# Setup copies and the written-out opening order of a fused forgetting-attention and GELU kernel

## Chip, cores and metric

The kernel runs on one core of one Trainium2 chip. The metric is the device time of one execution in microseconds (us), as the median over several executions; the span of a profiled execution goes from its first to its last instruction.

## What is computed

Attention with a forget gate for 8 batches, 8 heads, 576 positions and 64 columns a head, and then a two-layer network with a tanh-GELU on the 4608 x 512 result:

```python
scores = scale * q @ k.T                       # per head, 576 x 576
cum    = cumsum(log(clip(f, 1e-4, 1)))         # along the sequence
scores = where(j > i, -1e9, scores + cum[i] - cum[j])
attn   = softmax(scores)                       # along j
x      = (attn @ v) as 4608 x 512
out    = gelu_tanh(x @ w_in) @ w_out           # 512 -> 2048 -> 512
```

The decay of a row cancels in the softmax. So the kernel needs only a weight exp(-cum[j] - 64) for each key: it multiplies the rows of v by it, and the denominators are products with the column of weights.

## The kernel before

**Tiling.** Four heads make a quad, and there are 16 of them, two for each batch. For a quad, `scores` (L197) multiplies K and Q on TensorE with four 32-row groups side by side into PSUM (tile `ps_s`, pool of two buffers, shared with the first layer's `ps_h`). ScalarE takes the exponential into `pt` (L223). The diagonal blocks are then masked: by `mask` (L225) with GpSimd's affine selects, or by `mask_by_product` (L249) with VectorE, which multiplies by the triangles in `causal`. `denominators` (L292) multiplies `pt` by the weights `w_bf`, transposes, takes reciprocals and transposes again. `attn_out` (L310) multiplies `pt` by the weighted values `vw` and writes `xT`, normalised. `make_vw` (L173) makes `vw` from `v_nat` and `wT`, on GpSimd or VectorE. Quads 0 and 1 are cut into two parts of 256 and 320 query positions (`part` 0 and 1), so that the first layer can begin early.

**The network** works in nine chunks of 512 positions. `mlp_in` (L317) makes 256 of 2048 hidden columns of a chunk, and ScalarE applies the GELU. For chunk 0, `mlp_in_half` (L334) makes 512 hidden columns for one part of the positions. `mlp_out` (L352) is a generator: each step is one 128-row block of the hidden dimension into a block of 128 output rows, after the 16th VectorE copies the result out and SyncE stores it.

**Setup** (L374) issues the load of f on SyncE and the first two K and Q loads on GpSimd, makes an identity and an upper triangle `utri_f32` on GpSimd, and takes the logs of f on ScalarE. Five TensorE transposes put them into `ps_lt`, and two copies (L399, L400) into `logfT`. The running sums are matmuls of `logfT` by the triangle and by ones (`make_w`, L421). The second of them takes `before`, sums of whole blocks, which `sums_before` (L414, `SB`) makes on GpSimd. ScalarE's exponential of the sums gives `wT` (L426). `cast_w` (L445) makes the bf16 copy `w_bf`, and `triangles` (L409) the bf16 triangles.

**The order of the opening** is written out by hand in `FRONT` (L73). Each engine takes its instructions in the order in which the words stand, so a word that waits holds up what stands behind it on its engines. The words, with quad i, batch b, chunk c:

- `TK.i`, `TQ.i`: VectorE transposes of K and Q into `kT`, `qT`. `LK.i`, `LQ.i`: their loads, issued by GpSimd. A buffer holds every second quad.
- `LU.t`: the load of tile t (128 positions) of batch 0's v, all heads; `LV.b.half`: five loads for half of the heads of batch b. SyncE issues them. `WI.c`, `WO.c`: quarters of w_in and w_out, issued by GpSimd.
- `S.i.r`: scores of round r, all four heads; `H.i.r.g`: two of the heads. `M` and `m`: the masks on GpSimd and VectorE. `D.i.part`: denominators. `V.i.x.part`: a product with `vw` and the multiply into `xT`.
- `vw.i`, `VW.i`: `make_vw` on VectorE, GpSimd. `CL.i`: a copy inside `vw`. `CW`: `make_w`. `SB`: `sums_before`. `W`: `cast_w`. `TR`: `triangles`. `Z`: zero fills on GpSimd.
- `J.half.g`: `mlp_in_half`. `I.c.pr`: `mlp_in`. `F.c.n` and `f.c.n`: n steps of `mlp_out` of chunk c, in whole matmuls or, for `f`, as four matmuls of 32 rows.
- `B.n.cols`: n matmuls of zeros (`keep_busy`, L191), whose result nothing reads.
- `word@other`: the word's first DMA is issued only after the last DMA of `other` has landed; the issuing engine waits.

After `FRONT`, a loop over chunks 2 to 8 (L525) does the rest: each turn has the first layer of a chunk, the second layer of the one before, and the attention of two further quads. `TileContext` works out the semaphores; within an engine the order is that of the program (`manual_schedule`).

Of the kernel before, what the change touches and what calls it, by code (L numbers as in the profile page):

```python
# [16 lines left out]
def kernel(  # L17
# [10 lines left out]
    nc = tc.nc  # L28

    B, H, S, D = q.shape  # L30
    BH = B * H
    NT = (S + 127) // 128
# [34 lines left out]
    LOW, HIGH = NT, NT - 1  # L67
# [3 lines left out]
    """  # L71

    FRONT = """  # L73
        TK.0 TQ.0 TK.1 B.3.128 LU.4@LK.0 WO.0 SB CW TQ.1 W S.0.0 B.1.128 TR LU.0 B.4.256 M.0.0 B.2.384 S.0.2 B.4.256 H.1.0.1
        H.1.0.0 D.0.0 H.0.1.1 LU.1 vw.0.0 H.1.1.1 B.3.256 Z m.1.0 vw.1.0 H.0.1.0 LU.2@LK.0 WI.1 V.0.1.0 WI.0@LU.0 M.0.1 D.1.0 LU.3@LU.4 H.1.1.0 WI.3
        WI.2 V.0.0.0 LK.2 H.0.3.1 V.1.1.0 H.0.3.0 vw.0.1 m.0.3 V.1.0.0 H.1.3.0 H.1.3.1 D.0.1 H.1.2.0 M.1.1 M.1.3 LQ.2 H.1.2.1 V.0.0.1 V.0.1.1 D.1.1
        J.0.1 VW.1.1 V.1.1.1 WO.1@LU.3 WO.2 WO.3 LK.3 V.1.0.1 LV.1.1@WO.2 TQ.2 J.0.0 J.1.0 J.0.2 TK.2 J.1.2 J.1.1 J.0.3 J.1.3 F.0.6 LQ.3
        LV.1.0@LQ.3 LK.4 S.2.0 F.0.11 S.2.2 TQ.3 F.0.10 S.2.1 m.2.0 TK.3 TK.4 vw.3 F.0.10 LV.2.0 vw.2 M.2.2 CL.3 M.2.1 S.3.0 LQ.4
        CL.2 LQ.5 f.0.7 D.2 S.3.1 f.0.6 V.2.0 TQ.4 LK.5 S.3.2 f.0.7 m.3.0 V.2.1 S.4.1 F.0.5 H.4.2.1 M.3.1 M.3.2 D.3 H.4.0.0
        H.4.0.1 V.3.1 VW.4 v.3.0 LK.6 TQ.5 LV.3.0@LQ.3 f.0.2 LQ.6 H.4.2.0 TK.5 I.1.1 TK.6 LK.8 CL.4 I.1.6 LK.7 I.1.5 I.1.4 I.1.3  # L80
        m.4.0 I.1.2 I.1.0 I.1.7 F.1.8 M.4.1 TQ.6 S.5.0 LV.2.1@LK.7 M.4.2 f.1.7 VW.5 D.4 S.5.1 F.1.6 F.1.7 S.5.2 LV.3.1 LQ.7 m.5.1
        m.5.0 V.4.0 f.1.5 V.4.1 S.6.0 f.1.4 CL.5 vw.6 M.5.2 D.5 f.1.3 LQ.8 S.6.1 V.5.1 f.1.6 m.6.0 V.5.0 m.6.1 S.6.2 m.6.2
        CL.6 F.1.10
    """

    singles = ctx.enter_context(tc.tile_pool(name="singles", bufs=1))
# [6 lines left out]
    def many(n, shape, dtype, name):  # L93
        return [singles.tile(shape, dtype, name=f"{name}{i}") for i in range(n)]

    ident_f32 = singles.tile([BH, BH], FP32, name="ident_f32")
    utri_f32 = singles.tile([128, 128], FP32, name="utri_f32")
# [8 lines left out]
    vw = many(2, [128, NT + 1, 4, D], BF16, "vw")  # L106
# [6 lines left out]
    logfT = singles.tile([128, NT * BH], FP32, name="logfT")  # L113
    before = singles.tile([128, (NT - 1) * BH], FP32, name="before")
    wT = singles.tile([128, NQ, NT, 4], FP32, name="wT")
    w_bf = singles.tile([128, NQ, NT + 1, 4], BF16, name="w_bf")
    shift = singles.tile([128, 1], FP32, name="shift")
    idle = singles.tile([128, 512], BF16, name="idle")
    causal = many(2, [128, 128], BF16, "causal")


    def after(ins, other):

        tc.add_manual_dep(ins.ins, other.ins.name, mybir.DependencyInfo(
            mybir.DependencyClass.Sync, mybir.DependencyReason.DATA), reason="order of loads")

    def load_v(b, h0=0, nh=H, ts=range(NT)):
        ins = []
        for t in ts:
            n = min(128, S - 128 * t)  # L130
            ins.append(nc.sync.dma_start(
                out=v_nat[b % 2][:n, t, h0:h0 + nh, :],
                in_=v[b, h0:h0 + nh, 128 * t:128 * t + n, :].rearrange("h p d -> p h d"),
            ))
        return ins
# [16 lines left out]
    def load_one(src, dst, i):  # L152
        b, h0 = i // QPB, 4 * (i % QPB)
        return nc.gpsimd.dma_start(  # L154
            out=dst[i % 2].rearrange("p a d -> p (a d)"),
            in_=src[b, h0:h0 + 4].rearrange("h (p a) d -> (h p) (a d)", p=32))
# [217 lines left out]
    def setup():  # L374
        nc.sync.dma_start(out=f_sb, in_=f.rearrange("b h s -> (b h) s"))
        dmas["LK.0"] = load_one(k, k_c, 0)
        dmas["LQ.0"] = load_one(q, q_c, 0)
        make_identity(nc, ident_f32)
        dmas["LK.1"] = load_one(k, k_c, 1)
        dmas["LQ.1"] = load_one(q, q_c, 1)  # L380
        make_upper_triangular(nc, utri_f32, val=1.0, diag=True)

        nc.vector.memset(idle, 0.0)
        nc.vector.memset(ones_f32, 1.0)
        nc.vector.memset(logfT, 0.0)
        nc.vector.memset(shift, -64.0)
        nc.vector.memset(wT[64:128, :, HIGH, :], 0.0)
        for t_ in kT:
            nc.vector.memset(t_[:, 0:64], 0.0)
            nc.vector.memset(t_[:, 64 + S:], 0.0)  # L390
        nc.vector.tensor_scalar(f_sb, f_sb, 1e-4, 1.0, op0=ALU.max, op1=ALU.min)
        nc.scalar.activation(f_sb, f_sb, AF.Ln)
        idle_ps.append(psO.tile([128, 1024], FP32, name="idle_ps", tag="po"))
        ps_lt = psM.tile([128, NT * BH], FP32, name="ps_lt", tag="m")
        for t in range(NT):
            n = min(128, S - 128 * t)
            nc.tensor.transpose(ps_lt[:n, t * BH:(t + 1) * BH], f_sb[:, 128 * t:128 * t + n], ident_f32)
        run(SETUP)
        nc.vector.tensor_copy(logfT[:, :HIGH * BH], ps_lt[:, :HIGH * BH])  # L399
        nc.vector.tensor_copy(logfT[0:64, HIGH * BH:], ps_lt[0:64, HIGH * BH:])  # L400

    def zeros():
        for t_ in v_nat:
# [2 lines left out]
            nc.gpsimd.memset(t_[0:64, LOW, :, :], 0.0)  # L406
        nc.gpsimd.memset(w_bf[0:64, :, LOW, :], 0.0)

    def triangles():  # L409
        for m in causal:  # L410
            nc.vector.tensor_copy(m, utri_f32)
        nc.vector.tensor_copy(causal[1][64:128, 0:64], utri_f32[0:64, 0:64])

    def sums_before(eng):  # L414
        eng.tensor_copy(before[:, 0:BH], logfT[:, 0:BH])
# [23 lines left out]
    dmas = {}  # L439
# [2 lines left out]
        by_columns[:] = [True] * tiled  # L442
        pull(fills.setdefault(c, mlp_out(c)), n)

    def cast_w():  # L445
        nc.vector.tensor_copy(w_bf[:, :, 0:NT, :], wT)
        nc.vector.tensor_copy(w_bf[64:128, :, LOW, :], wT[0:64, :, 0, :])

    def load_values(b, half):
        return load_v(b, 4 * half, 4)  # L450

    ops = {
        "W": cast_w,
        "CW": make_w,
        "SB": lambda: sums_before(nc.gpsimd),
        "sb": lambda: sums_before(nc.vector),
        "Z": zeros,
        "TR": triangles,
        "S": lambda i, r: scores(i, r),
        "H": lambda i, r, g: scores(i, r, ((2 * g, 2 * g + 1),)),  # L460
        "M": lambda i, r, *keys: mask(i, r, keys),
# [10 lines left out]
        "LQ": lambda i: load_one(q, q_c, i),  # L472
        "LV": load_values,
        "LU": lambda t: load_v(0, ts=(t,)),
        "WI": load_w_in,
        "WO": load_w_out,
        "I": lambda c, pr: mlp_in(c, (pr,)),
# [6 lines left out]
    def run(table):  # L484

        for word in table.split():
            word, _, gate = word.partition("@")
            name, *args = word.split(".")
            did = ops[name](*map(int, args))
            did = did if isinstance(did, list) else [did]  # L490
            if gate:
                after(did[0], dmas[gate])
            dmas[word] = did[-1]

    def step(i, j, c, n):

# [25 lines left out]
    with tc.manual_schedule():  # L522
        setup()
        run(FRONT)
        for c in range(2, NCH):  # L525
            for pr in range(2):
                mlp_in(c, (pr,))
            out_part(c - 1, CH)
            if c + 1 < B:
                prepare(2 * c + 3, 2 * c + 4)  # L530
            if c + 2 < B:
                load_v(c + 2)
            for pr in range(2, NP):
# [37 lines left out]
```

## Time and profile before

| | |
|---|---|
| median of nine runs | 349.76 us (343.11 to 355.57) |
| the nine runs | 343.11, 344.15, 344.72, 344.78, 349.76, 350.85, 352.25, 355.29, 355.57 |
| the profiled execution: its own time, its span | 344.17 us, 342.5 us |
| mean granted TensorE clock of the profiled execution | 0.990 |
| DMA | 33.25 MB in 50999 packets, 38992 of them under 512 B |

The page has one line for the busy time of each engine (PE is TensorE's matmuls, PEld its weight loads, DVE VectorE, ACT ScalarE, POOL GpSimd, SP SyncE) and then the span in 40 slices of 8.6 us; a digit is the busy share in tenths. PEclk is the clock granted to TensorE, in tenths of full speed. A line of waits tells who waited for whom, the total in us, how often, and the longest. A line of the table by stretches has the stretch, its length, the busy time of PE, PEld, DVE, ACT and POOL with the number of instructions, the clock, the busy share of the 16 DMA engines (over 1 where packets overlap) and the GB/s that they moved.

### The profile page before, as it was taken

The page shows a single profiled execution, that of the slowest core. Times are in us where ns is not written, and L with a number is a line of the kernel's source. Part 1 is how long each engine was busy: PE and PEld are TensorE (multiplying, and loading weights), DVE is VectorE, ACT ScalarE, POOL GpSimd, SP SyncE. Part 2 cuts the span into 40 slices and gives each one's busy share as a digit, 9 for nine tenths or more (in the row PEclk, how much of TensorE's full clock was granted, in tenths as well). Part 3 has the DMA queues.
Part 4 walks back from the last instruction along what each step waited for, and adds up shares of the span by engine and source line. Part 5 has one row for each costly group of instructions (what it writes and reads, how often), then busy time and mean ns, then how long its engine had stood idle before and what let it go on. Part 6 is the DMA issues. An engine that isn't in the chain of part 4 may idle for free.

```text
span 342.5 us, 9365 instructions
## 1 busy us (share of the span) xinstructions
PE 331.8 (97%) x4221; PEld 163.0 (48%) x4221; DVE 135.7 (40%) x209; ACT 190.8 (56%) x192; POOL 91.4 (27%) x131
## 2 busy tenths in 40 slices
PE   4999999999999999999999999999999999999995
PEld 2448834544454454444444444444444544444443
DVE  5785139670575235343425243514530450011011
ACT  3874576776665566557574667466745714510500
POOL 6565014442110135321642055106500410000000
PEclk9969999999999999999999999999999999999999
DMA  7999975984532930096007710560100010002012
GB/s 129 212 198 200 208 184 108 202 147 92 129 74 70 215 86 34 33 206 134 34 33 166 142 65 33 110 130 33 65 31 2 33 63 32 0 33 83 9 47 77
DMA packets 50999, 33.25 MB, mean 97 GB/s; under 512 B 38992, under 2 KB 41296, under 8 KB 50960
## 3 DMA queue, kind: packets, MB, share of 16 engines
q0 software_dynamic: 7808, 13.63, 23.0%
q1 hardware_dynamic: 43008, 18.96, 20.9%
q8 instruction: 33, 0.54, 0.6%
q10 hardware_dynamic: 144, 0.07, 0.1%
q14 instruction: 6, 0.05, 0.0%
HBM read 36.85 MB, written 9.44 MB: 135 GB/s over the span
## 4 chain that ended last, share of the span: by engine, by line
PE 83%; POOL 1%; ACT 1%; issue 0%; POOLq 0%; DVE 0%
PE pso L363 35%; PE ps_h L325 32%; PE po L283 8%; PE ps_s L215 7%; POOL vw L177 1%; ACT pt L223 1%; PE ps_o L283 0%; POOL pt L229 0%; POOLq L566 0%; DVE o_st L368 0%; POOLq L229 0%
## 5 line engine op out<-in xcount | busy, mean ns | idle before, releaser
L363 PE MATMUL pso<-w_out_sb,gT 128*32 128x512 bf16 (+2 forms) x1483 | 134.7, 377 | 0.0
L223 ACT ACTIVATE pt<-ps_s 128x1024 bf16<-128x1024 f32 (+2 forms) x100 | 94.0, 991 | 39.4 <-PE ps_s L215 36.9
L325 PE MATMUL ps_h<-xT,w_in_sb 128*128 128x512 bf16 x512 | 112.9, 379 | 0.0
L332 ACT ACTIVATE gT<-ps_h 128x1024 bf16<-128x1024 f32 x64 | 65.5, 1023 | 76.2 <-PE ps_h L325 76.2
L363 PEld LDWEIGHTS <-gT 128*32 128x32 bf16 (+1 forms) x1483 | 56.5, 97 | 56.9 <-issue 2.4
L325 PEld LDWEIGHTS <-w_in_sb 128*128 128x128 bf16 x512 | 49.6, 98 | 61.4 <-issue 2.5
L229 POOL TENSOR_SCALAR_AFFINE_SELECT pt<-pt 128x512 bf16<-128x512 bf16 (+3 forms) x62 | 37.6, 617 | 122.1 <-ACT pt L223 120.8
L368 DVE COPY o_st<-pso 128x512 f32<-128x512 f32 (+2 forms) x37 | 24.9, 674 | 90.2 <-PE pso L363 90.0
L215 PE MATMUL ps_s<-qT,kT 32*128 32x64 bf16 (+5 forms) x896 | 37.7, 268 | 0.9 <-ACT pt L223 0.6
L302 DVE STREAM_TRANSPOSE den<-po 128x576 f32<-128x576 f32 x14 | 11.0, 782 | 62.0 <-PE po L283 62.0
L314 DVE TENSOR_TENSOR xT<-po,rb 128x576 bf16<-128x576 f32 x26 | 19.7, 757 | 29.6 <-PE po L283 29.4
L177 POOL TENSOR_TENSOR vw<-v_nat,wT 128x1280 bf16<-128x1280 f32 (+1 forms) x12 | 27.1, 2259 | 9.9 <-DMA v_nat<-in_v_dram 7.0
L215 PEld LDWEIGHTS <-kT 32*128 32x128 bf16 x896 | 17.5, 94 | 24.6 <-issue 19.6
L283 PE MATMUL po<-pt,vw 128*32 128x64 bf16 (+4 forms) x624 | 22.5, 279 | 0.0
L154 POOL DMA_DIRECT2D k_c<-in_k_dram x16 | 9.1, 567 | 46.4 <-DVE kT L160 41.3
L160 DVE STREAM_TRANSPOSE qT<-q_c 128x576 f32<-128x576 f32 x16 | 19.9, 1244 | 2.5 <-DMA q_c<-in_q_dram 2.4
L160 DVE STREAM_TRANSPOSE kT<-k_c 128x576 f32<-128x576 f32 x16 | 19.9, 1243 | 2.3 <-PE ps_s L215 1.3
L283 PEld LDWEIGHTS <-vw 128*32 128x32 bf16 x672 | 14.0, 97 | 11.8 <-issue 4.6
L342 PE MATMUL ps_h<-xT,w_in_sb 128*128 128x256 bf16 x128 | 14.3, 273 | 0.0
L342 PEld LDWEIGHTS <-w_in_sb 128*128 128x128 bf16 x128 | 12.4, 98 | 1.6
L306 DVE STREAM_TRANSPOSE rb<-rec 128x576 f32<-128x576 f32 (+2 forms) x18 | 12.8, 712 | 0.6
L349 ACT ACTIVATE gT<-ps_h 128x1024 bf16<-128x1024 f32 x8 | 8.2, 1023 | 8.2 <-PE ps_h L342 8.2
(59 smaller groups left out, 118.0 us busy)
## 6 DMA issues: line engine op xcount, KB each, us to landing
out_dram<-o_st SPq DMA_DIRECT2D x35, 256.0 KB, 2.1
v_nat<-in_v_dram SPq DMA_DIRECT2D x20, 256.0 KB, 8.1
k_c<-in_k_dram POOLq DMA_DIRECT2D x16, 288.0 KB, 6.4
q_c<-in_q_dram POOLq DMA_DIRECT2D x16, 288.0 KB, 7.5
v_nat<-in_v_dram SPq DMA_DIRECT2D x29, 128.0 KB, 4.9
w_out_sb<-in_moe_w_out_dram POOLq DMA_DIRECT2D x4, 512.0 KB, 9.9
w_in_sb<-in_moe_w_in_dram POOLq DMA_DIRECT2D x4, 512.0 KB, 8.4
v_nat<-in_v_dram SPq DMA_DIRECT2D x6, 64.0 KB, 3.2
```

The source lines that it names most:

```text
L160: nc.vector.transpose(out=dst.rearrange("p s c -> p (s c)").bitcast(FP32) .rearrange("p (t a) -> p a t", a=S // 32), in_=src.rearrange("p ...
L177: eng.tensor_mul(vw[i % 2][:, t0:t1], vb[:, t0:t1, h0:h0 + 4, :], wT[:, i, t0:t1, :].unsqueeze(3).to_broadcast([128, t1 - t0, 4, D]))
L215: nc.tensor.matmul(tiles[h // 2][:, h % 2, c0:c0 + nq], key_columns(i, key, h, c), qq[32 * h:32 * h + 32, q0:q0 + nq, c], start=(c == 0 an ...
L223: nc.scalar.activation(p[:, 2 * g:2 * g + 2, off:off + n], t[:, :, 0:n], AF.Exp, scale=scale)
L229: nc.gpsimd.affine_select(out=x, in_=x, compare_op=ALU.is_ge, fill=0.0, base=0, pattern=pattern, channel_multiplier=-1)
L283: nc.tensor.matmul(po[r0:r0 + w.shape[-1], 448 + q0:448 + q0 + nq], w, p[:, h, col:col + nq], start=(key in (0, "low")), stop=(key in ("lo ...
L314: nc.vector.tensor_mul(xT[:, 2 * u + x, S * b + s0:S * b + s1], po, rbs[i, part])
L325: nc.tensor.matmul(ph[:, j, :], w_in_sb[:, dt, 128 * ft:128 * ft + 128], xT[:, dt, CH * c:CH * (c + 1)], start=(dt == 0), stop=(dt == N_DT ...
L332: nc.scalar.activation(gT[c % 2][:, 2 * pr:2 * pr + 2, :], ph, AF.Gelu_apprx_tanh)
L342: nc.tensor.matmul(ph[:, j // 2, QA * (j % 2):QA * (j % 2) + QA], w_in_sb[:, dt, 128 * ft:128 * ft + 128], xT[:, dt, n0:n0 + QA], start=(d ...
L363: nc.tensor.matmul(pso[c0:c0 + cols, m0:m1], gT[c % 2][:, ft, 128 * n + c0:128 * n + c0 + cols], w_out_sb[:, ft, m0:m1], start=(ft == 0), ...
L368: nc.vector.tensor_copy(st[:, m0:m1], pso[:, m0:m1])
```

## The change

The logs' two copies out of PSUM are issued on ScalarE. A word `w` makes `cast_w` on ScalarE, and the new `FRONT` uses it in the place of `W`. A word `tr` makes `triangles` on ScalarE; the new `FRONT` has it nowhere, its triangles are made by `TR`, on VectorE, as the first word. A word `LP` would load a tile of v from GpSimd's queue; it isn't used either. `FRONT` is another order of nearly the same words. The work is the same but for the fillers `B`, the split of some rounds (`S.1.2` for `H.1.2.0 H.1.2.1`, `H.4.1.1 H.4.1.0` for `S.4.1`), the engine of some masks and of `vw.4`, `vw.5`, and the gates of some loads.

```diff
     FRONT = """
-        TK.0 TQ.0 TK.1 B.3.128 LU.4@LK.0 WO.0 SB CW TQ.1 W S.0.0 B.1.128 TR LU.0 B.4.256 M.0.0 B.2.384 S.0.2 B.4.256 H.1.0.1
-        H.1.0.0 D.0.0 H.0.1.1 LU.1 vw.0.0 H.1.1.1 B.3.256 Z m.1.0 vw.1.0 H.0.1.0 LU.2@LK.0 WI.1 V.0.1.0 WI.0@LU.0 M.0.1 D.1.0 LU.3@LU.4 H.1.1.0 WI.3
-        WI.2 V.0.0.0 LK.2 H.0.3.1 V.1.1.0 H.0.3.0 vw.0.1 m.0.3 V.1.0.0 H.1.3.0 H.1.3.1 D.0.1 H.1.2.0 M.1.1 M.1.3 LQ.2 H.1.2.1 V.0.0.1 V.0.1.1 D.1.1
-        J.0.1 VW.1.1 V.1.1.1 WO.1@LU.3 WO.2 WO.3 LK.3 V.1.0.1 LV.1.1@WO.2 TQ.2 J.0.0 J.1.0 J.0.2 TK.2 J.1.2 J.1.1 J.0.3 J.1.3 F.0.6 LQ.3
-        LV.1.0@LQ.3 LK.4 S.2.0 F.0.11 S.2.2 TQ.3 F.0.10 S.2.1 m.2.0 TK.3 TK.4 vw.3 F.0.10 LV.2.0 vw.2 M.2.2 CL.3 M.2.1 S.3.0 LQ.4
-        CL.2 LQ.5 f.0.7 D.2 S.3.1 f.0.6 V.2.0 TQ.4 LK.5 S.3.2 f.0.7 m.3.0 V.2.1 S.4.1 F.0.5 H.4.2.1 M.3.1 M.3.2 D.3 H.4.0.0
-        H.4.0.1 V.3.1 VW.4 v.3.0 LK.6 TQ.5 LV.3.0@LQ.3 f.0.2 LQ.6 H.4.2.0 TK.5 I.1.1 TK.6 LK.8 CL.4 I.1.6 LK.7 I.1.5 I.1.4 I.1.3
-        m.4.0 I.1.2 I.1.0 I.1.7 F.1.8 M.4.1 TQ.6 S.5.0 LV.2.1@LK.7 M.4.2 f.1.7 VW.5 D.4 S.5.1 F.1.6 F.1.7 S.5.2 LV.3.1 LQ.7 m.5.1
-        m.5.0 V.4.0 f.1.5 V.4.1 S.6.0 f.1.4 CL.5 vw.6 M.5.2 D.5 f.1.3 LQ.8 S.6.1 V.5.1 f.1.6 m.6.0 V.5.0 m.6.1 S.6.2 m.6.2
-        CL.6 F.1.10
+        TR TK.0 WO.0@LK.0 SB TQ.0 TK.1 LU.4@LK.0 CW S.0.0 TQ.1 B.1.384 M.0.0 B.5.384 w S.0.2 B.4.256 LU.1 H.1.0.1 D.0.0 LU.0@LQ.1
+        Z H.1.0.0 H.0.1.1 vw.0.0 B.2.256 WI.1 H.1.1.1 V.0.1.0 H.0.1.0 WI.0@LU.0 m.1.0 vw.1.0 M.0.1 WI.3 V.0.0.0 H.1.1.0 B.4.128 D.1.0 LU.3 H.0.3.1
+        LU.2 V.1.1.0 H.0.3.0 V.1.0.0 WI.2 H.1.3.0 H.1.3.1 LK.2 m.0.3 vw.0.1 D.0.1 S.1.2 V.0.0.1 LK.3 m.1.3 m.1.1 V.0.1.1 J.0.1 D.1.1 VW.1.1
+        V.1.1.1 LQ.2 V.1.0.1 TK.3 WO.1@LU.3 WO.2@LK.3 LV.1.1@WO.2 LV.1.0 TK.2 WO.3 TQ.2 J.0.0 LQ.3 J.1.0 J.0.2 J.0.3 J.1.1 TQ.3 J.1.3 J.1.2
+        F.0.6 LK.4 S.2.0 F.0.12 S.2.2 F.0.10 S.2.1 TK.4 vw.3 F.0.10 M.2.0 S.3.0 vw.2 CL.2 M.2.2 M.2.1 LQ.4 LK.5 LK.6 f.0.7
+        D.2 S.3.1 f.0.7 V.2.0 LQ.5 S.3.2 TQ.4 CL.3 F.0.5 V.2.1 H.4.1.1 H.4.1.0 M.3.0 F.0.4 m.3.1 H.4.2.1 LV.2.0 m.3.2 TK.5 D.3
+        H.4.0.0 H.4.0.1 V.3.1 f.0.1 LV.2.1@LQ.3 v.3.0 LK.7 f.0.2 H.4.2.0 I.1.1 LV.3.0@LV.2.1 I.1.5 vw.4 I.1.7 I.1.3 I.1.0 I.1.4 vw.5 M.4.0 I.1.2
+        TQ.5 LQ.6 I.1.6 F.1.7 TK.6 LV.3.1@LQ.6 M.4.2 S.5.0 TQ.6 M.4.1 f.1.8 D.4 S.5.1 F.1.12 CL.4 S.5.2 LK.8 LQ.7 M.5.1 V.4.0
+        f.1.6 V.4.1 S.6.0 M.5.0 f.1.3 CL.5 M.5.2 D.5 f.1.4 S.6.1 V.5.1 m.6.0 f.1.6 V.5.0 LQ.8 S.6.2 M.6.1 vw.6 m.6.2 CL.6
+        F.1.10
     """
...
-        nc.vector.tensor_copy(logfT[:, :HIGH * BH], ps_lt[:, :HIGH * BH])
-        nc.vector.tensor_copy(logfT[0:64, HIGH * BH:], ps_lt[0:64, HIGH * BH:])
+        nc.scalar.copy(logfT[:, :HIGH * BH], ps_lt[:, :HIGH * BH])
+        nc.scalar.copy(logfT[0:64, HIGH * BH:], ps_lt[0:64, HIGH * BH:])
...
-    def triangles():
+    def triangles(copy):
         for m in causal:
-            nc.vector.tensor_copy(m, utri_f32)
-        nc.vector.tensor_copy(causal[1][64:128, 0:64], utri_f32[0:64, 0:64])
+            copy(m, utri_f32)
+        copy(causal[1][64:128, 0:64], utri_f32[0:64, 0:64])
...
-    def cast_w():
-        nc.vector.tensor_copy(w_bf[:, :, 0:NT, :], wT)
-        nc.vector.tensor_copy(w_bf[64:128, :, LOW, :], wT[0:64, :, 0, :])
+    def cast_w(copy):
+        copy(w_bf[:, :, 0:NT, :], wT)
+        copy(w_bf[64:128, :, LOW, :], wT[0:64, :, 0, :])
...
-        "W": cast_w,
+        "W": lambda: cast_w(nc.vector.tensor_copy),
+        "w": lambda: cast_w(nc.scalar.copy),
...
-        "TR": triangles,
+        "TR": lambda: triangles(nc.vector.tensor_copy),
+        "tr": lambda: triangles(nc.scalar.copy),
...
+        "LP": lambda t: load_v(0, ts=(t,), eng=nc.gpsimd),
...
-            dmas[word] = did[-1]
+            dmas[word.replace("LP.", "LU.")] = did[-1]
```

More of the change, by code (lines that the diff above doesn't have):

```diff
@@ L125, in after, with load_v @@
             mybir.DependencyClass.Sync, mybir.DependencyReason.DATA), reason="order of loads")
-    def load_v(b, h0=0, nh=H, ts=range(NT)):
+    def load_v(b, h0=0, nh=H, ts=range(NT), eng=nc.sync):
         ins = []
@@ L130, in load_v @@
             n = min(128, S - 128 * t)
-            ins.append(nc.sync.dma_start(
+            ins.append(eng.dma_start(
                 out=v_nat[b % 2][:n, t, h0:h0 + nh, :],
```

## Prediction

> **What bounds the kernel now.** I read the page's busy shares and its forty slices first, then the waits of the opening, then the opening in equal stretches. The page:
>
> ```profile
> span 342.5 us, 9365 instructions
> PE 331.8 (97%) x4221; PEld 163.0 (48%) x4221; DVE 135.7 (40%) x209; ACT 190.8 (56%) x192; POOL 91.4 (27%) x131
> ...
> PE   4999999999999999999999999999999999999995
> ...
> PEclk9969999999999999999999999999999999999999
> DMA  7999975984532930096007710560100010002012
> ```
>
> TensorE is busy everywhere, but a busy share is no proof of speed: in slice 3 (17 to 26 us) the granted clock is 0.6. The DMA engines are full for the first six slices. The same in stretches of one period of the clock's record (us; sum; then PE, PEld, DVE, ACT, POOL busy; clock; DMA share; GB/s):
>
> ```profile
> 9.40:12.80 3.40, 3.40 (x30) 1.41 (x19) 3.23 (x5) 2.28 (x5) 1.39 (x3) 1.00 1.17 190
> 12.80:16.20 3.40, 3.22 (x47) 1.81 (x47) 2.16 (x6) 3.33 (x6) 3.00 (x7) 1.00 1.28 244
> 16.20:19.60 3.40, 2.57 (x48) 1.33 (x44) 2.93 (x8) 2.42 (x3) 1.69 (x3) 1.00 1.18 215
> 19.60:23.00 3.40, 3.40 (x52) 1.54 (x52) 2.96 (x7) 2.70 (x5) 2.05 (x4) 0.50 1.11 201
> 23.00:26.40 3.40, 3.40 (x68) 1.81 (x60) 2.08 (x6) 2.58 (x4) 2.62 (x4) 0.50 1.07 170
> 26.40:29.90 3.50, 3.50 (x80) 2.70 (x76) 1.98 (x5) 1.58 (x2) 3.50 (x6) 0.99 1.09 202
> 29.90:43.00 13.10, 13.10 (x128) 11.37 (x121) 3.08 (x4) 6.78 (x8) 0.75 (x2) 1.00 1.19 207
> ```
>
> The stretch with a hole in PE (2.57 of 3.40) is followed by two at half clock. From 26.4 PE has no hole, apart from 0.6 us at 47.7. So everything after about 30 us is a fixed amount of PE work, and the front changes the total only through the moment at which PE gets there. The waits between 8.8 and 30 us:
>
> ```profile
> ACT pt L223 <- PE ps_s L215: 3.6, 6, 1.0
> ...
> DVE vw L177 <- DMA v_nat<-in_v_dram: 1.5, 2, 1.1
> ...
> PEld L269 <- DVE vw L177: 0.9, 1, 0.9
> PE po_m L269 <- DVE vw L177: 0.6, 1, 0.6
> ```
>
> In that stretch ScalarE's exponentials pace the work (13.4 us busy from 8.84 to 25.79, 3.6 us of gaps). The longest gap, 0.98 us at 17.87, is that of the first `V`: it waits for `vw.0.0`, which waits for a tile of v landing at 16.5.
>
> **What the Trainium skill says.** "TensorE: Matmul & The Clock Gate", section "Part 1: The HAM clock gate", says that the clock is halved after a window of some 3.4 us with too little PE work and given back after a busy one, and that the windows run free of the kernel. The trace agrees: the half clock lasts 6.83 us, two such windows. "ScalarE: Activation LUTs", section "What ACT_TABLE_LOAD costs", prices an ACTIVATE with immediate scale and bias at 186 ns + 0.833 ns an element; its section "Table sets" says that copies lie in every set, so none needs a table load of its own. No copy on ScalarE is in this trace; its exponential of 128x1024 is 1.0 us, near the page's 1.04. "DMA: Bandwidth & Descriptors", section "Queues, rings and completion order", says that the DMA engines take turns between queues packet by packet. Here v's 256-byte packets on SP's queue hardly move until POOL's queue runs dry at 14.0 us; then a tile of v lands each 1.1 us (14.3, 15.3, 16.5, 17.7).
>
> **The change, part by part.**
>
> *Logs.* VectorE's two copies (0.42 and 0.21, both done 5.61 to 6.16) go to ScalarE. By the skill's price 0.40 and 0.24, overlapped some 0.55: done at about 6.15 again. If the table load of 4.67 to 5.95 stays ahead of them, they end at 6.5, +0.35 for the sums; if it falls behind them it runs beside the sums, with 2.9 us of ScalarE idle there. I take 0; ends 0 and +0.35.
>
> *Triangles.* Despite the change's words they stay on VectorE (`TR`, not `tr`), now first: 1.18 us (12.72 to 13.90) from 4.65, when the triangle is made, to 5.84. K's transpose then starts at 5.84 for 6.08, but Q's still waits for its load (landed 7.57) and ends at 8.86. Worth 0. Gone from 12.72, they free the first denominators, which waited 0.2 us behind them; D's result isn't wanted before 17.7. Worth 0.
>
> *`WO.0` waits for the first K load* (landed 5.58). Behind it on POOL stands `SB`. The issue takes 0.77 us, so `SB` starts at 6.37 for 6.10: the last sum matmul, held by `SB`, moves from 7.58 to 7.84 and ends at 9.05 for 8.80. The first scores start at 9.1 for 8.91 (Q's transpose was just as late): **+0.2**. Its data don't move, since K and Q of the second four heads are ahead of it in the queue until 10.6.
>
> *`w` on ScalarE.* Two copies, 0.45 and 0.24 by the page's price, about 0.6, after the first scores' exponentials. ScalarE idles 0.86 us just there: hidden. Without that gap it would be +0.6; VectorE loses 0.92 us that nobody waited for.
>
> *Fillers.* After the first scores `B.1.384 B.5.384`, 2304 columns, for 1920. At the trace's 0.89 ns a column there (1.71 us from 9.67 to 11.38) 2.05 us: `S.0.2` starts at 11.9 for 11.38, its exponential at 12.65 for 12.14. **+0.5 in all so far**, since ScalarE then runs without gap.
>
> *`V.0.1.0` ahead of `H.0.1.0`.* The load of tile 0 of v is now third instead of second, gated on q's second load (10.6). By the rate above the third tile lands at 16.5, where the later of the two needed landed before. So `V.0.1.0` still starts at 17.35, but PE's queue holds `H.0.1.0` behind it: issued at 16.09 before, at 17.7 after. ScalarE ends `H.1.1.1` at 17.46 and sits idle until 18.37; then `H.0.1.0` and `H.1.1.0` follow, ending at 20.2 for 19.76. **+0.45 in all.** The hole in PE grows from some 0.6 to 1.3 us, so the clock still falls at 19.6. `WI.0` waits for that tile too: issued at 16.5 for 15.6, with the queue backed up to 21.7 (`WI.1`'s landing): 0. The DMA issues queued behind it stay ahead of their data.
>
> *The second round.* `S.1.2` takes the two halves `H.1.2.0`, `H.1.2.1` together: it needs both score buffers, so ScalarE idles some 0.8 us. Placing the six exponentials by their rows (0.76, last two 0.65) and scores at half clock at 0.7: the last ends at 27.3 for 25.79. But PE then has `V.0.0.1`, `V.0.1.1` (from 25.9, the clock back at 26.45: to 27.2), and `J.0.1`, now ahead of `D.1.1`, 1.74 to 29.0; it covers the last masks, which go from POOL to VectorE (three, some 1.1 us, done by 28.1). `D.1.1` and two products (0.65, 1.15): 30.8 for 30.05. **+0.75.**
>
> *After that.* K, Q, w_out and v for later quads move a place or two in queues that are full until 45 us; each lands before its use (`WO.1` 37 for 42.3, `LQ.3` 43.4 for the scores at 53.4). `TQ.3` blocks VectorE until 44.7, ahead of an output copy of 46.7: 0. `F.0.12` for `F.0.11` puts one matmul of 0.23 into the hole of 0.6 at 47.7: **-0.2**. `vw.4` and `vw.5` go from POOL (2.26 us each) to VectorE (1.48) behind 14 us of PE's first-layer block: 0; `LV.2.0` leaves some 6 us later, 61 for 55, wanted at 68: 0. Split scores and shuffled fillers keep their sums (64 and 56 matmul steps in either).
>
> *Sum*: +0.75 - 0.2 = **+0.55**. The profiled execution took 344.17 (span 342.5, 1.7 around it): 344.7. The median shown, 349.76, lies 5.6 above it: **350.3**. The nine runs fall in two groups, 343.1 to 344.8 (four) and 349.8 to 355.6 (five), the profile in the lower; its place in the clock's windows is one of many.
>
> **Rivals.**
> *The clock (slower).* With the larger hole, and a window that begins elsewhere, one more 6.83 us at half clock falls on the first-layer pieces after 26 us, which are PE work without slack: +3.4, so 353.7. It decides if half clock reaches beyond 28. For it: two stretches with PE full stayed at 0.50. Against: `B.4.128` and `J.0.1` come early and fill.
> *Tile 0 lands late (slower).* It is issued at 10.65, not 6.29. A v tile took at least 6.67 us from issue to landing here, so 17.3 to 18.2: up to 1.7 late, and every later score stands behind it: 352.0. Decides from a landing past 17.5. Against: that time was queueing.
> *The clock holds (faster).* Longer early fillers warm PE surely and `J.0.1` keeps it so: without half clock PE saves some 2.6 us (1.5 of ScalarE's gaps after 19.6, 1.1 of the two products), and one of nine runs changing groups moves the median to the lower one: 344.8 + 0.55 = 345.3. For it: the median is next to the gap between groups.
> *It does not do what it says*: true of the triangles; priced above at 0.
>
> **How the numbers follow.** Little change 0.35; clock slower 0.22; late tile 0.15; clock holds 0.28. A run-to-run spread like the one shown can tell about 0.5% (1.75 us) from no change, so faster 0.28, same 0.35, slower 0.37; the little-change case alone spans 348.5 to 351.5 with the unknown copies (+0.35 for the load order, -0.5 if the fillers run warm). The range reaches into both other cases: 344.4 to 354.5.
>
> **What would show it.** Right: ScalarE's copies at 5.6 and in the gap near 11.5, no added table load; `SB` at 6.4; first scores at 9.1; no score between 16.0 and 17.7; the last exponential of the pair near 27.3, `J.0.0` at 30.8; a hole of about 0.4 near 47.7. Wrong: tile 0 landing past 17.5, half clock elsewhere than 19.6 to 26.5, a table load before a copy, or a new hole after 31 us.

## The result, and the profile after

The changed kernel takes 346.95 us as the median of 16 runs (346.5 to 347.72). In the same comparison the kernel before has a median of 346.46 (51 runs, 342.15 to 355.68), and the ratio is 1.0069, with a 95% interval of 1.0049 to 1.0088. The ratio leaves out executions more than 1.5% above the fastest of their kernel, which for the kernel before are 24 of the 51; what sets those apart is a subject of its own below. Against the executions that are left, the change costs about 0.7%; but its own spread is 1.2 us, where that of the kernel before is 13.5. The forecast of 350.3 was 3.35 too high, with both of its parts wrong: the trace lost more than the sum said (2.2 us more), and the offset added to it (some 5.5 too much) was no property of the changed kernel. That 346.95 lies within the stated 344.4 to 354.5 is owed to the width of that range and to two errors of opposite sign, so in part to luck.

The profiled execution took 346.90, with a span of 345.2 (before 344.17 and 342.5). The page after, the lines that answer to those shown of before:

```profile
span 345.2 us, 9348 instructions
PE 332.7 (96%) x4211; PEld 162.7 (47%) x4211; DVE 137.3 (40%) x207; ACT 192.0 (56%) x196; POOL 89.6 (26%) x133
...
PE   3799999999999999999999999999999999999996
...
PEclk9958999999999999999999999999999999999999
DMA  7999994989130960077105911370100010001002
```

Slice 3 of the clock fell from 0.6 to 0.5 and slice 4 from full to 0.8: half clock lasts longer. What goes before it is seen in the same stretches as before (stretch, length, PE, PEld, DVE, ACT and POOL busy, clock, DMA share, GB/s):

```profile
16.20:19.60 3.40, 2.12 (x32) 0.97 (x32) 2.40 (x6) 1.72 (x2) 0.71 (x1) 0.79 0.94 171
19.60:23.00 3.40, 3.40 (x48) 1.39 (x44) 1.83 (x5) 1.97 (x3) 3.29 (x6) 0.50 1.13 207
23.00:26.40 3.40, 3.40 (x56) 1.49 (x52) 2.98 (x6) 2.22 (x4) 2.59 (x3) 0.50 1.08 166
26.40:29.90 3.50, 3.50 (x54) 2.50 (x47) 2.37 (x7) 2.55 (x3) 0.00 (x0) 0.72 1.10 190
```

PE is busy 2.12 us where it was 2.57, and half clock runs from 18.15 to 28.39: three windows of 3.41, where before there were two (19.63 to 26.45). The waits between 8.8 and 30 us, and PE's timeline, name the hole:

```profile
ACT pt L223 <- PE ps_s L215: 4.3, 6, 1.6
...
PE po_m L269 <- DVE vw L177: 1.7, 1, 1.7
...
17.48 0.35 PE L269 MATMUL po_m<-pt,vw 128*32 128x256 bf16 x8 [1.68 <-DVE vw L177]
```

Where did the time come from? I compared the starts of all GELUs in the two traces. The lag is 2.18 us at the second of them and stays at that to the sixteenth (82.77 before, 84.95 after); at the seventeenth (104.86, 107.97) it is 3.11, and from there it creeps to 3.18. The end of the program takes back 0.45. So the span's 2.73 has two sources: **2.18 in the first 32 us, and 0.93 between 85 and 108 us**, where the forecast had priced everything at nothing.

The second source is found by reading ScalarE around 85 us. Before:

```profile
82.77 1.02 ACT L332 ACTIVATE gT<-ps_h 128x1024 bf16<-128x1024 f32 x1 [0.70 <-PE ps_h L325]
83.81 1.28 ACT L223 ACT_TABLE_LOAD   x1
85.13 1.94 ACT L223 ACTIVATE pt<-ps_s 128x1024 bf16<-128x1024 f32 x2
```

After:

```profile
84.95 1.02 ACT L332 ACTIVATE gT<-ps_h 128x1024 bf16<-128x1024 f32 x1 [0.70 <-PE ps_h L325]
...
87.16 1.28 ACT L223 ACT_TABLE_LOAD   x1 [1.18 <-PE ps_s L215]
88.45 1.94 ACT L223 ACTIVATE pt<-ps_s 128x1024 bf16<-128x1024 f32 x2
...
90.44 0.63 PE L215 MATMUL ps_s<-qT,kT 32*128 32x64 bf16 x14 [0.71 <-ACT pt L223]
```

Before, the table load of the first exponential after the GELUs starts when the last GELU ends. After, it first waits 1.18 us for the scores, and only then loads: what lay beside the scores now follows them, and 0.71 of it reaches PE as a wait for a free score buffer.

### The profile page after: what moved, and what is told of

It is laid out like the page before. It is cut to its first block, busy times and chain, and to the rows that moved or that the text cites. A ratio compares the mean times of both kernels' runs of the same rounds, so it can differ in the third digit from the quotient of the medians.

```text
span 345.2 us, 9348 instructions
## 1 busy us (share of the span) xinstructions
PE 332.7 (96%) x4211; PEld 162.7 (47%) x4211; DVE 137.3 (40%) x207; ACT 192.0 (56%) x196; POOL 89.6 (26%) x133
## 4 chain that ended last, share of the span: by engine, by line
PE 81%; ACT 1%; POOL 1%; issue 1%; POOLq 0%; DVE 0%; ACTq 0%
PE pso L363 33%; PE ps_h L325 32%; PE po L283 8%; PE ps_s L215 7%; ACT pt L223 1%; POOL vw L177 1%; PE ps_o L283 0%; POOL pt L229 0%; POOLq L569 0%; DVE o_st L368 0%; ACT L223 0%; ACTq L223 0%; POOLq L229 0%
## 5 line engine op out<-in xcount | busy, mean ns | idle before, releaser
L229 POOL TENSOR_SCALAR_AFFINE_SELECT pt<-pt 128x512 bf16<-128x512 bf16 (+2 forms) x66 | 40.4, 620 | 128.1 <-ACT pt L223 126.6
L215 PE MATMUL ps_s<-qT,kT 32*128 32x64 bf16 (+5 forms) x896 | 38.6, 270 | 1.6 <-ACT pt L223 1.6
L177 POOL TENSOR_TENSOR vw<-v_nat,wT 128x1280 bf16<-128x1280 f32 (+1 forms) x10 | 22.4, 2242 | 0.0
```

The source lines that it names most:

```text
L177: eng.tensor_mul(vw[i % 2][:, t0:t1], vb[:, t0:t1, h0:h0 + 4, :], wT[:, i, t0:t1, :].unsqueeze(3).to_broadcast([128, t1 - t0, 4, D]))
L215: nc.tensor.matmul(tiles[h // 2][:, h % 2, c0:c0 + nq], key_columns(i, key, h, c), qq[32 * h:32 * h + 32, q0:q0 + nq, c], start=(c == 0 an ...
L229: nc.gpsimd.affine_select(out=x, in_=x, compare_op=ALU.is_ge, fill=0.0, base=0, pattern=pattern, channel_multiplier=-1)
```

## The experiments

A figure "at n windows" below is a mean over the runs with n windows of half clock. The number is read from a run's mean granted clock: 0.990 means that 2% of some 343 us, 6.9 us, ran at half speed, which is two windows; 0.985 is three, 0.980 four. For the kernel before it is a mean over the 148 executions with a recorded clock that ran beside the variants, on three chips: 38 have two windows, 33 three, 70 four or more. The median of the kernel before was between 345.65 and 349.64 in these comparisons, so variants of its order are better compared at equal windows.

**Undoing the product's move**, in the changed kernel.

```diff
-H.1.1.1 V.0.1.0 H.0.1.0 WI.0@LU.0
+H.1.1.1 H.0.1.0 V.0.1.0 WI.0@LU.0
```

> The changed kernel with H.0.1.0 put back ahead of V.0.1.0. Theory of the hole: PE's queue held a score behind a product that waits for v until 17.5, which left ScalarE without work for 1.64 us and PE empty for 1.68 us. With the score in front the hole shrinks to about 0.6, the ninth exponential starts near 16.9 instead of 18.5, J.0.0 starts near 30.3 instead of 32.2, and the time falls by 1.5 to 2 us, to about 345. Rival, that S.1.2 in one piece and the order of J.0.1 and D.1.1 cost the time: the gain is under 0.5 us.

Measured: 346.32 (344.68 to 346.77, 20 runs), ratio to the kernel before 1.0024 (1.0003 to 1.0045). The profiled span is 343.8, 1.45 shorter than after. The ninth exponential starts at 17.32 for 18.54, half clock is two windows again (19.77 to 26.60), and the second GELU comes 1.46 earlier. So the hole theory holds in this trace, for 1.45 of the 2.18. Over all runs it is worth less, 0.6 in the median and 1.0 in the mean. The profiled run, 345.45, is the fastest of seven with two windows, and their mean of 346.4 is no better than that of the eight with three (346.3); only the five with one window are clearly faster (345.1). What the move changes is the number of windows: the changed kernel has three in 15 of its 16 runs. The two traces also differ in when the clock's windows begin (one at 12.95 here, at 11.32 after), so the pair alone does not part the hole from the clock's phase.

**Undoing the masks of quad 3**, in the changed kernel: two from VectorE back to GpSimd, one the other way.

```diff
-M.3.0 F.0.4 m.3.1 H.4.2.1 LV.2.0 m.3.2
+m.3.0 F.0.4 M.3.1 H.4.2.1 LV.2.0 M.3.2
```

> The changed kernel with quad 3's masks on the engines that they had before (round 0 on VectorE, rounds 1 and 2 on GpSimd). Theory of the table load: the exponential of S.5.0 waits for more semaphores, so the load of its table stands behind the wait for the scores. With the old masks the load waits for VectorE alone, runs right after the last GELU, the exponential starts 1.2 us earlier and the time falls by 0.9 us, to about 346.0. Rival, that the later loads or the shuffled fillers near 85 us cost the 0.9: no change.

Measured: 346.0 (345.42 to 346.93, 20 runs), ratio 1.0040 (1.0022 to 1.0057). At three windows the mean is 346.01, 0.95 less than the 346.96 of the changed kernel. The lag of the GELUs stays 2.15 through the whole trace; the step of 0.93 is gone. The same place as above:

```profile
84.92 1.02 ACT L332 ACTIVATE gT<-ps_h 128x1024 bf16<-128x1024 f32 x1 [0.70 <-PE ps_h L325]
85.96 1.28 ACT L223 ACT_TABLE_LOAD   x1
87.25 1.94 ACT L223 ACTIVATE pt<-ps_s 128x1024 bf16<-128x1024 f32 x2
```

**The same masks alone**, in the kernel before.

```diff
-m.3.0 V.2.1 S.4.1 F.0.5 H.4.2.1 M.3.1 M.3.2
+M.3.0 V.2.1 S.4.1 F.0.5 H.4.2.1 m.3.1 m.3.2
```

> The kernel before with nothing changed but the engines of quad 3's masks (round 0 to GpSimd, rounds 1 and 2 to VectorE, as the change has them). Theory of the table load: the load near 83.8 now stands behind the wait for the scores, and everything after 85 us comes 0.9 us later; about +0.9 in the fast runs. Rival: the shift comes from another part, and nothing moves.

Measured: 348.68 (344.0 to 357.61, 20 runs), ratio 1.0039 (1.0000 to 1.0078). The median is blurred by the spread of this order, but the mean at three windows is 346.77 for the 345.53 of the kernel before, +1.2. The trace has the load behind the wait, and the lag grows by 1.15 there:

```profile
88.76 1.28 ACT L223 ACT_TABLE_LOAD   x1 [1.40 <-PE ps_s L215]
90.06 1.94 ACT L223 ACTIVATE pt<-ps_s 128x1024 bf16<-128x1024 f32 x2
```

Undone in one kernel it goes, done alone in the other it comes: that is shown. The programs differ at this point in what the load waits for, VectorE alone before and in the run with the masks undone, TensorE and ScalarE in the other two. That the masks' engines decide it through the waits that the exponential needs fits both runs; how the two are put in order in the program was not tried further.

**The product's move alone**, in the kernel before.

```diff
-vw.1.0 H.0.1.0 LU.2@LK.0 WI.1 V.0.1.0 WI.0@LU.0
+vw.1.0 LU.2@LK.0 WI.1 V.0.1.0 H.0.1.0 WI.0@LU.0
```

> The kernel before with V.0.1.0 moved ahead of H.0.1.0, as the change has it, and nothing else. Theory of the hole: the score waits behind the product, the ninth exponential comes 1.2 to 1.7 us later (near 18.3 for 16.84), PE's hole grows from 0.6 to some 1.5 us, and J.0.0 starts 0.8 to 2 us later, so at the same length of half clock the time is 1 to 1.5 us longer (near 345.5 where two windows are at half clock, for 344.15). Rival, that the hole costs only together with the fillers and S.1.2 of the change: under 0.5 us at the same length of half clock.

Measured: 347.75 (345.32 to 355.19, 20 runs), ratio 1.0074 (1.0028 to 1.0120). The ninth exponential is 1.86 late, but two further on only 0.66 is left; at three windows the mean is 345.58, no different from the 345.53 of before. What it changed is how often: no run had two windows, where 38 of the 148 executions of the kernel before did (seven of 35 beside this run). That fits a hole that is paid through the clock and hardly by itself.

**The copies alone**, in the kernel before: the logs and the bf16 weights by ScalarE.

```diff
-        nc.vector.tensor_copy(logfT[:, :HIGH * BH], ps_lt[:, :HIGH * BH])
-        nc.vector.tensor_copy(logfT[0:64, HIGH * BH:], ps_lt[0:64, HIGH * BH:])
+        nc.scalar.copy(logfT[:, :HIGH * BH], ps_lt[:, :HIGH * BH])
+        nc.scalar.copy(logfT[0:64, HIGH * BH:], ps_lt[0:64, HIGH * BH:])
...
-        nc.vector.tensor_copy(w_bf[:, :, 0:NT, :], wT)
-        nc.vector.tensor_copy(w_bf[64:128, :, LOW, :], wT[0:64, :, 0, :])
+        nc.scalar.copy(w_bf[:, :, 0:NT, :], wT)
+        nc.scalar.copy(w_bf[64:128, :, LOW, :], wT[0:64, :, 0, :])
...
-TQ.1 W S.0.0 B.1.128
+TQ.1 S.0.0 W B.1.128
```

> The kernel before with the logs' copies and the bf16 weights on ScalarE (the weights after the first exponentials), in its own order. By the prediction these copies lie in gaps of ScalarE: the exponentials before 17 us stay within 0.2 us of their times, and at the same length of half clock the time is within 0.5 us of the kernel before. Rival, that the copies push the exponentials: the third starts 0.6 us later and the time follows.

Measured: 350.65 (349.66 to 353.56, four runs), ratio 1.0168 (1.0078 to 1.0259). For the copies this decides nothing: the exponentials before 17 us are 0.15 to 0.43 earlier, and the time is lost later, in two waits for other things:

```profile
DVE vw L177 <- DMA v_nat<-in_v_dram: 6.0, 1, 6.0
PE po_m L269 <- DVE pt L258: 5.9, 1, 5.9
```

The last tile of v landed at 27.37, for 20.99 in the profile of before. VectorE's `vw.0.1` waits for it, the masks `m.0.3` stand behind that, and PE's `D.0.1` waits for the masks. This line of waits led to the next question: is it what spreads the times of the kernel before?

**The late tile.** In the kernel before, `vw.0.1` put behind the masks:

```diff
-H.0.3.0 vw.0.1 m.0.3 V.1.0.0
+H.0.3.0 m.0.3 V.1.0.0 vw.0.1
```

> The kernel before with vw.0.1 moved behind m.0.3 and V.1.0.0 in VectorE's queue, and nothing else. In the profiles of its variants the last tile of v landed at 21.0, 23.6, 24.3 and 27.4 us; VectorE waited for it in vw.0.1, with the mask m.0.3 behind it, PE's D.0.1 waited for the mask, and the last two exponentials of the pair came 3 to 5 us after the landing. Theory of the late tile: with the mask and V.1.0.0 in front, D.0.1 no longer waits for the tile, landings up to 24.5 cost nothing, and the spread shrinks from 342 to 356 to about 343.5 to 349, median near 345. Rival, that the spread comes from the clock's windows alone, whatever lands when: the spread and the median stay at 342 to 356 and 348.

Measured: 345.63 (344.2 to 352.77, 20 runs), ratio 1.0018 (0.9992 to 1.0043). Five of 20 runs had four windows or more, where 70 of the 148 of the kernel before have, 23 of 50 beside this run. The spread shrinks, but a tail remains, and 20 runs leave the size of the gain open. The profile caught a run of the tail, with the tile landing at 28.25, later than even the moved `vw.0.1` can bear. In the changed kernel, the old gate and the old order brought back:

```diff
-LU.3 H.0.3.1 LU.2 V.1.1.0
+LU.3 H.0.3.1 LU.2@LU.4 V.1.1.0
...
-m.0.3 vw.0.1 D.0.1
+vw.0.1 m.0.3 D.0.1
```

> The changed kernel with vw.0.1 put back ahead of m.0.3 and the last tile's load (LU.2 here) gated on LU.4, as the last tile of the kernel before was. Theory of the late tile: the wide spread comes back, some runs at 349 and more, with D.0.1 waiting for the mask behind vw.0.1. Rival, that the changed kernel's steadiness comes from its fixed hole and J.0.1's place: all runs stay between 346.5 and 348.

Measured: 347.27 (346.88 to 349.5, 15 runs), ratio 1.0078 (1.0055 to 1.0100). Two of 15 runs have four windows, 348.75 and 349.5; the changed kernel and the others with its order and without this edit have none in 112 runs. So the two edits bring a little of the tail back. They did not bring back the late tile: `LU.4` had landed at 13.49, the gate held the issue only to 13.57, and in this profile the tile landed at 18.61. What a late tile costs in the changed kernel is therefore not shown. What this profile lost is another wait: `vw.0.1` took 3.19 us, beside a product on GpSimd (the hold described below), and PE waited 2.6 for the masks behind it.

The link between tile and time rests on the profiles of the old order. With the front of before the last tile of v is issued from 0.7 us ahead of `WI.1` on POOL's queue to 1.05 behind it, and lands at 20.99, 23.63, 24.33, 27.37 and 28.25. In the first four of these, where `vw.0.1` still stands ahead of the masks, PE's longest wait for the masks is none, 1.5, 2.5 and 5.9 us, and the execution has two, four, four and five windows of half clock. With the changed front it is issued 0.4 to 1.7 us ahead, at 13.05 to 14.06, and lands at 18.3 to 21.8. The eight profiles with a lead above 0.75 took 5.0 to 6.4 us from issue to landing, the six with less or with a lag 6.7 to 13.1. Within the six the lead does not order them: 0.19 took 6.7, 0.70 took 9.6, a lag of 0.07 took 13.1. So the lead is a clue, and what decides is not shown.

**`D.1.1` ahead of `J.0.1`**, in the changed kernel, to see whether the early first-layer piece is what steadies the times.

```diff
-V.0.1.1 J.0.1 D.1.1 VW.1.1
+V.0.1.1 D.1.1 J.0.1 VW.1.1
```

> The changed kernel with D.1.1 put back ahead of J.0.1. The runs of the changed kernel all have three windows of half clock, those of the kernel before from none to eight. Theory: J.0.1, dense work for PE, now comes before the denominators and gives the clock back after the third window; with D.1.1 in front, which waits for the masks, PE has a hole near 27, some runs get a fourth or fifth window, and these take 349 us and more, the others about 347. Rival, that the large hole near 16 fixes the number of windows by itself: still three windows in all runs, 347 to 347.5.

Measured: 346.82 (345.8 to 347.26, 14 runs), ratio 1.0045 (1.0026 to 1.0064), still with no run above three windows. The piece's place is not the reason.

**Filling the hole.** In the changed kernel, seven filler matmuls ahead of the product:

```diff
-H.1.1.1 V.0.1.0 H.0.1.0
+H.1.1.1 B.7.512 V.0.1.0 H.0.1.0
```

> The changed kernel with seven matmuls of zeros of 512 columns (1.5 us at full clock) ahead of V.0.1.0, into the hole of 1.68 us. If most of the loss is the clock that falls after the hole: no half clock at 18.1, PE saves up to 3 us by J.0.0, time about 344.5. If the loss is only that scores come late for ScalarE: the exponentials stay where they are until 21, and the time stays within 0.5 us of 346.9.

Measured: 346.7 (343.61 to 348.66, 12 runs), ratio 1.0028 (0.9983 to 1.0073). A miss, and a useful one. The clock was full from 12.21 to 25.86 and the exponentials at 22 us came 2.03 earlier than after. Then all of it was lost. In the timeline of VectorE and of POOL, and in the waits:

```profile
22.15 2.76 DVE L258 TENSOR_TENSOR pt<-pt,causal 128x512 bf16<-128x512 bf16 x2
...
22.93 1.48 POOL L177 TENSOR_TENSOR vw<-v_nat,wT 128x768 bf16<-128x768 f32 x1
...
PE po_m L269 <- DVE pt L258: 1.7, 1, 1.7
```

Before, the same two mask products, `m.0.3`, take 0.61:

```profile
22.40 0.61 DVE L258 TENSOR_TENSOR pt<-pt,causal 128x512 bf16<-128x512 bf16 x2
```

It is the first of the two that is held: it runs from 22.15 to 24.70 and ends 0.29 after POOL's `VW.1.1`, which ends at 24.41. PE waits 1.69 for the masks, and the clock falls at 25.86. The Trainium skill has this in "SBUF — State Buffer", section "SBUF: two separate sides": a VectorE operation with two inputs in SBUF and a GpSimd operation that reads SBUF exclude each other, and the one that starts first keeps the other out until it is done. The trace agrees that they exclude each other: after, where `m.0.3` begins during `VW.1.1`, it too ends 0.29 behind it (24.59 for 24.30). It does not agree on the order: here the mask product started 0.78 before `VW.1.1` by the records (22.15 for 22.93) and was the one held. Starts on POOL are rough figures; why it came second stays open.

**The combination**: the masks undone, a shorter filler, and `VW.1.1` with `V.1.1.1` behind two loads on POOL's queue.

```diff
-H.1.1.1 V.0.1.0 H.0.1.0
+H.1.1.1 B.5.512 V.0.1.0 H.0.1.0
...
-D.1.1 VW.1.1 V.1.1.1 LQ.2 V.1.0.1 TK.3 WO.1@LU.3
+D.1.1 LQ.2 WO.1@LU.3 VW.1.1 V.1.1.1 V.1.0.1 TK.3
```

> The changed kernel with three edits: quad 3's masks back on their old engines, five matmuls of zeros of 512 columns in the hole ahead of V.0.1.0, and VW.1.1 on GpSimd after LQ.2 and WO.1. With the seven fillers alone the exponentials up to 24 us came 2 us earlier, but then the second instruction of the mask m.0.3 on VectorE took until GpSimd's VW.1.1 was done (2.8 us for two that take 0.6) and the gain was lost. Theory: the mask is held by the GpSimd product; with VW.1.1 later it takes 0.6, J.0.0 starts 1.5 to 2.5 us earlier than in the changed kernel, and with 0.9 from the masks the time is 343.5 to 344.5. Rival, that the loads of w_in (WI.0 landing near 24.1) or tile 2 of v are the next bound: J.0.0 within 0.5 us of the changed kernel, 346.0.

Measured: 342.41 (342.33 to 343.09, six runs), ratio 0.9919 (0.9890 to 0.9949). In these runs it is faster than both kernels, and all six runs are without half clock after the opening. Its stretches, laid along its clock's windows:

```profile
12.05:15.46 3.41, 2.98 (x46) 1.48 (x38) 1.10 (x3) 3.03 (x5) 3.00 (x8) 1.00 1.26 236
15.46:18.87 3.41, 3.20 (x45) 1.53 (x45) 1.81 (x5) 2.31 (x3) 0.71 (x1) 1.00 1.25 214
18.87:22.29 3.42, 3.23 (x68) 1.62 (x68) 3.23 (x9) 3.40 (x5) 2.83 (x5) 1.00 1.12 209
...
21.80 0.63 DVE L258 TENSOR_TENSOR pt<-pt,causal 128x512 bf16<-128x512 bf16 x2
```

The two mask products, `m.0.3`, take 0.63, and the second GELU starts at 30.55, 3.64 ahead of after. What filler and `VW.1.1` give each by itself was not separated; the run with the filler alone suggests that the first needs the second.

**The combination with the copies on VectorE again.**

```diff
-        nc.scalar.copy(logfT[:, :HIGH * BH], ps_lt[:, :HIGH * BH])
-        nc.scalar.copy(logfT[0:64, HIGH * BH:], ps_lt[0:64, HIGH * BH:])
+        nc.vector.tensor_copy(logfT[:, :HIGH * BH], ps_lt[:, :HIGH * BH])
+        nc.vector.tensor_copy(logfT[0:64, HIGH * BH:], ps_lt[0:64, HIGH * BH:])
...
-B.5.384 w S.0.2
+B.5.384 W S.0.2
```

> The combination (masks back, five fillers in the hole, VW.1.1 later) with the logs' copies and the bf16 weights put back on VectorE. It has no late tile and no half clock, so the copies show by themselves. Prediction's step: they are worth nothing either way, the time stays within 0.3 us of the combination's 342.4. Rival, that ScalarE's copies free VectorE for something that matters: 0.5 us or more slower.

Measured: 342.85 (342.14 to 343.32, 12 runs), ratio 0.9938 (0.9914 to 0.9963). Against the combination that is +0.25 in the mean, 342.78 for 342.53, well inside the two kernels' spreads; by these spreads the difference is known to about 0.3, and the two ran on different chips. What names the change shows no gain beyond that, a few tenths of a microsecond at most.

**The combination with the score first and two fillers.**

```diff
-H.1.1.1 B.5.512 V.0.1.0 H.0.1.0
+H.1.1.1 H.0.1.0 B.2.512 V.0.1.0
```

> The combination with H.0.1.0 put back ahead of V.0.1.0 and two matmuls of zeros of 512 columns between them instead of the five. Theory of the hole: ScalarE's gap of 1.1 us ahead of the ninth exponential closes (17.2 for 18.3), J.0.0 starts 0.5 to 1 us earlier, 341.4 to 341.9. Rival, that w_in (WI.0 landing at 24.0) is the next bound for J.0.1: within 0.3 us of 342.4.

Measured: 345.17 (343.3 to 346.19, 12 runs), ratio 0.9976 (0.9937 to 1.0014). The ninth exponential starts at 16.76, 1.5 ahead of the combination, and still 2.8 are lost:

```profile
18.15:21.56 3.41, 2.87 (x56) 1.46 (x53) 3.24 (x8) 2.39 (x3) 3.41 (x7) 1.00 1.11 204
21.56:24.98 3.42, 2.88 (x44) 1.14 (x43) 3.42 (x6) 1.80 (x3) 2.37 (x2) 0.50 1.11 171
24.98:28.39 3.41, 3.41 (x51) 2.22 (x48) 2.89 (x8) 2.58 (x3) 0.00 (x0) 0.50 1.04 149
```

PE is busy 2.87 in the window ahead of the fall, where the combination has 3.2 in its own windows. But the clock is not all of it. The three of the 12 runs without half clock have a mean of 343.97, still 1.4 above the combination. In this order POOL's queue runs ahead as well, so that `VW.1.1` starts at 22.30 (23.83 in the combination) and `m.0.3` is held beside it once more:

```profile
21.96 2.12 DVE L258 TENSOR_TENSOR pt<-pt,causal 128x512 bf16<-128x512 bf16 x2
...
22.30 1.62 POOL L177 TENSOR_TENSOR vw<-v_nat,wT 128x768 bf16<-128x768 f32 x1
```

What the clock and the hold cost each was not separated, so this run does not say what serving ScalarE at once is worth by itself.

## Why the prediction was right and wrong

**Setup: right.** The copies out of PSUM take 0.37 and 0.20, those of the weights 0.46 and 0.24 (forecast 0.40, 0.24, 0.45, 0.24), and the table load falls behind the first two, beside the sums. The changed kernel's ScalarE:

```profile
5.81 0.37 ACT L399 COPY logfT<-ps_lt 128x256 f32<-128x256 f32 x1 [0.95 <-PE ps_lt L397]
6.08 0.20 ACT L400 COPY logfT<-ps_lt 64x64 f32<-64x64 f32 x1
6.30 1.28 ACT L426 ACT_TABLE_LOAD   x1
...
11.33 0.46 ACT L446 CAST w_bf<-wT 128x320 bf16<-128x320 f32 x1
```

`SB` starts at 6.41 (forecast 6.37), the first scores at 9.07 (9.1), the first exponential 0.17 later than before (+0.2). No table load was added. That the copies cost nothing stands on the pair of combinations, to some 0.3. The triangles took 0.59 (4.87 to 5.46) where the forecast had 1.18; both are worth nothing.

**Fillers: "+0.5 in all so far" did not show.** The third exponential starts at 12.12 for 12.14. In this execution the clock was full from 11.32, for 12.80 before, so the fillers ran at full speed: the case that the forecast kept in its range as "if the fillers run warm". In the profiles of variants with the changed opening the same exponential is 0.28 to 0.52 late where the clock came at 12.0 to 13.0, and 0.73 to 1.20 late where it came at 14.6 to 14.9; of this 0.11 to 0.88 is there at the first exponential already, ahead of the fillers.

**"+0.45 in all" for the product: too small, the term was mis-sized.** The tile landed at 16.61 (forecast 16.5) and the product started at 17.48 (17.35), so the wait was as described. ScalarE, not delayed by the fillers, was done at 16.89 and stood 1.64, not 0.9, but the exponential behind that gap started at 18.54, only 0.17 after the forecast 18.37. What the term missed comes next: the scores of the following exponential ran at half clock already (1.03 us from 18.87, where they took 0.63 before), so that one is 1.09 late, and all behind it are 1.88 late.

**"The clock still falls at 19.6" and "the clock back at 26.45": the step that failed.** It fell at 18.15 and came back at 28.39. `V.0.0.1` and `V.0.1.1`, which the forecast had at full clock from 26.45 and done at 27.2, started at 26.27, ran 2.22 us at half clock and ended at 28.4; the last exponentials had ended at 27.67 (27.3). `J.0.0` followed at 32.23 for the forecast 30.8. This is the rival of the slower clock, whose turning point ("if half clock reaches beyond 28") was met, though it cost 1.4 on top of the forecast +0.75 and not 3.4: the extra window fell, as far as the traces tell, on work that partly waited for ScalarE anyway. Part of the earlier fall is the clock's phase: its windows begin at 11.32 in this execution, at 12.80 in that of before. The third window is not: with windows from 12.08, the run with the masks undone has it too (18.91 to 29.15). That the hole brings the fall is seen best in the last run, whose windows begin as after (11.30 and 11.32): with the score first and two fillers in the hole, PE is busy 2.95 in the window to 18.15, and the clock holds until 21.55. The undoing run agrees in its trace, less so in its other runs.

**Masks moved between engines: priced at nothing, cost 0.93.** The forecast took everything after about 30 us for a fixed amount of PE work; at 90.44 PE waits 0.71 for a score buffer. It moved quad 3's masks without a word; it asked who would be late for the masks, and not what else depends on their engine. Shown by two runs.

**Late tile 0: no.** 16.61, as the sum had it. **`F.0.12`: right.** The hole near 50 us is 0.42 for 0.60, -0.18 for the forecast -0.2.

**The trace's sum** was +0.55; it was +2.73.

**The median's offset: the largest error.** The forecast carried the 5.6 us between profile and median of the kernel before over to the changed one and put it down to the clock's phase. The profile of the kernel before was a good execution of a kernel with a long tail: its mean is 344.2 at two windows, 345.5 at three, 349.8 at four, 352.2 at five, 354.7 at six. Four profiles point to the last tile of v for that tail: the later it lands, the longer PE stands, and the longer half clock lasts. In the old order its issue falls just around that of `WI.1`, and the reordered front issues it earlier. No run made the tile late in a steady kernel, and the run that took the masks out of its way kept part of the tail, so how much of the tail is the tile's stays open. All but one of the 16 executions of the changed kernel have three windows, and its profile lies in the middle of its runs. At three windows it is 1.4 slower than the kernel before (346.96 for 345.53); over all executions of the comparison with it, it is 1.4 faster in the mean (347.0 for 348.4). So "slower by 0.4% at like clock" and "faster on average" are both true, of different questions. Each program was profiled once, so how far apart two executions of one program issue that tile, and why, stays open.

## What to carry to other kernels

A stall of TensorE can be paid twice, as the wait and as the windows at half speed after it: price it with the clock, and add up the work in each window of the clock rather than look at the longest gap. Filling a hole is worth nothing where what comes earlier then collides with something else, as the mask did. When a step moves to another engine, look at every instruction that waits for that step, and at a table load ahead of one of them. And when runs spread, find what differs between a good and a bad execution before adding the spread to a forecast; a transfer issued within a microsecond of a large one in another queue is a place to look.

## What the runs showed of the hardware

**The clock.** A hole of 1.68 us was enough for half clock (after):

```profile
14.74:18.15 3.41, 1.73 (x30) 0.82 (x26) 1.11 (x3) 2.16 (x3) 1.15 (x2) 1.00 0.95 178
```

The Trainium skill, "TensorE: Matmul & The Clock Gate", section "HAM oscillation — how this bites in real kernels", warns of idle gaps above some 3.4 us; here gaps of half that, or several small ones, were enough. Busy time does not tell which windows are enough: one at 2.87 of 3.41 was followed by a fall (the combination with the score first), and in three other traces windows at 2.59 to 2.80, between 87 and 94 us, kept the clock.

What parts them in all 14 profiles is another sum: of each matmul that starts in the window, the columns that it moves, times the share of the 128x128 array that its weights fill. A score or a product with 32 rows or 32 columns of weights counts a quarter, a filler or a first-layer matmul in full. Laid along each trace's own changes of the clock, from its first full clock to 330 us, the 13 windows at full clock that were followed by a fall have at most 2756 such columns, and the 1265 others at least 2980. Before, the window ahead of the fall has 2276, after 1872, the combination with the score first 2692; the combination has 3396 or more in all of its windows. At half clock, 18 windows with at most 2498 were followed by another, and 11 with at least 2844 by full clock; two windows of one profile (the one with `vw.0.1` moved) ended half clock at 2044 and 2460. This is found in the traces after the fact, and no run was made to test it. It would explain why fillers keep the clock where the same time of attention work does not.

**Loads.** The same 256 KB load took from 5.0 to 13.1 us to land while its issue moved by 2.6 us (13.05 to 15.63) against another queue's.

**VectorE beside GpSimd.** A product of two SBUF tiles on VectorE that takes 0.42 us by itself took 2.55 beside GpSimd's product and ended 0.29 after it, though it had started first by the records.
